# A gated SSM/MLP kernel: deeper buffer rings for the last stage, and a re-planned order of all engines

## The chip, the cores and the metric

The kernel runs on one core of a Trainium2 chip. The metric is the time of one execution in device microseconds (us), lower is better: the median of 8 runs. Beside it there is one execution that was profiled by the hardware; all durations below come from that one.

## What is computed

A token sequence of 2048 rows and 640 columns, `A_q`, goes through two branches that are mixed by a gate per row. Cut to what matters:

```python
g = sigmoid((A_q * gate_w).sum(-1))
# branch A: long convolution of kv with ssm_k, by FFT
k_shift = sum of 4 shifted copies of A_k, each times a column of A_shift_k
kv = k_shift * A_v
y  = irfft(rfft(kv padded) * rfft(ssm_k padded))[:2048] + kv * ssm_D
a  = A_q * y
# branch B: token-shift mixer, then an MLP
h  = gelu(layernorm(A_q) @ w1)
x1 = A_q + shifted(h) @ w2          # quarters of h shifted by +1, -1, +2, -2 rows
b  = x1 + gelu(layernorm(x1) @ w3) @ w4
out = g * a + (1 - g) * b
```

## The kernel before

The rows are held as 128 partitions times 16 slabs (slab `s` is a [128 x 640] tile). The FFT is written as matmuls with tables, in two steps with a trip through DRAM between them, because the second step needs the rows in another layout.

The work is cut into some 600 nodes with names. `ORDER` (line 85 of the file) is one long string that lists all of them, each with its engine and the number of the ring slot for each of its buffers: `y0/V/1/0` is node `y0` on VectorE with slot 1 of one ring and slot 0 of another. A ring is a small set of buffers; a node that takes a slot waits until the last user of that slot is done. The string was written by a planner that is not part of the kernel. The kernel just emits the nodes in this order, so that **each engine executes its own nodes in the order of the string**, one after the other, and a node that waits holds up everything behind it on its engine. P is TensorE, V is VectorE (DVE), A is ScalarE (ACT), G is GpSimd (POOL), S is SyncE (SP), which issues all DMAs.

The nodes that the text speaks of, with the lines of the profile:

- `st`, `rs`, `xn`, `xt` (L497 to L537): layer norm. `st` takes statistics (VectorE, or ScalarE L503), `rs` on POOL (L516 to L523) makes the factor, `xn` normalises (VectorE, L530), `xt` is a transposing DMA (L537).
- `W1`, `g1` (L574, L581), `mx` (L609 to L614, copies of a 32-partition part for the shifts), `W2`, `add` (L663, L670): the mixer. `W3`, `g2` (L749, L753), `W4`, `w4e` (L762, L768): the MLP in four chunks of 512 rows; `w4e` adds (1 - g) times the product into the slab `QX[:, s]`. `xo` scales `QX` by (1 - g) ahead of it (VectorE L682 or ScalarE L684).
- `h1`, `he`, `hw` and `x1`, `xe`, `xw`: the first step of the transform of `ssm_k` and of `kv` (L718, copies L320/L324, DMA to DRAM L727). `km`, `ka`, `kv` (L806, L811, L815, L818): the shifted products on VectorE that make `kv`; they read 1280 elements per partition from each of two SBUF operands.
- `m3i0` to `m3i5`, `m3b`, **`m3c`** (16 small POOL instructions, L432 to L448), **`m3d`** (VectorE, L452), `m3s` (ScalarE sine, L454), `m3n` (POOL, L456): a chain that computes the small table for the second step. `w4` (the load of W4, L733) and `tri` wait for `m3n`.
- `rh`, `rx` (DMA L862, back from DRAM), `h2`, `x2`, `pv` (TensorE L835), `h2e`, `x2e`, `ve` (copies out of PSUM), `sw` (DMA L878), `pq` (VectorE product L895), `vw` (DMA to DRAM L912): the second step, the product of the spectra and the inverse's first step, in four chunks of five.
- The **tail**: `rv` (L919) reads the inverse's input back from DRAM, eight DMAs of 640 KB; `rq` (L923) loads `A_q` again, eight of 320 KB; for each slab `iv` (TensorE, 4 matmuls, L931), `ye` (ScalarE, L941, PSUM to SBUF times g), `y` (VectorE, times q, L945), `ya` (VectorE, adds it into `QX`, L951) and `st` (DMA to the output, L953). `rv0` waits for all four `vw`.

In the tail `rv` has a ring of 4 slots, `rq` of 2, and the product buffer `GY` (written by `ye`) of 4. The last `W3`/`W4` nodes are put between the nodes of the trip to DRAM and of the tail, to fill TensorE.

Of the kernel before, what the change touches and what calls it, by code (L numbers as in the profile page):

```python
# [109 lines left out]
km0.1.1/V/0/0 km0.1.0/V/0/1 xo3/A ka0.1.1/V/0/0 m3i1/G mx2.3/G W2.6/P/6 ka0.1.0/V/1/0 add6/V/6 xt1.0.1/S/0/1 w3/S h1.8.0/P/0/2  # L110
he.8.0/A/0/2 kv2/V/0 W2.7/P/4 add7/V/4 m3c/G m3d/V m3s/A W2.9/P/2 add9/V/2 mx3.2/G xt1.0.2/S/0/0 W2.8/P/0 xt1.0.3/S/0/2
W3.0.7/P/6/0/0 g2.0.7/A/6/0 W3.0.8/P/7/0/1 g2.0.8/A/7/1 xo5/A add8/V/0 h1.15.0/P/4/0 W3.0.3/P/0/0/2 W3.0.4/P/1/0/0
W3.0.9/P/6/0/1 g2.0.4/A/1/0 he.15.0/A/4/0 W3.0.2/P/7/0/2 W3.0.5/P/1/0/0 g2.0.5/A/1/0 g2.0.9/A/6/1 st1.6/A mx3.3/G k1/S/1
# [874 lines left out]
```

## Time and profile before

| what | value |
|---|---|
| median of 8 runs (lowest, highest) | 232.05 us (229.82, 235.35) |
| the profiled execution's own time | 230.78 us |
| its span in the profile | 229.0 us |
| TensorE busy | 213.0 us, 93% of the span |
| VectorE, ScalarE, POOL busy | 189.3, 165.3, 60.8 us |
| granted TensorE clock | 0.99 of full speed |
| bytes moved by DMA | 65.9 MB, 288 GB/s on average |

The span runs from the first to the last instruction of the profile; the execution's own time has 1.8 us around it. The page divides the span into 40 slices with a digit for the busy share of each, follows the chain of work that ended last back from the end, and lists groups of equal instructions with the idle time before them and what ended it. A wait is named as "engine line waited for: total us, times, longest". The mean length of a matmul includes its way through the array; from one start to the next, 128x512 matmuls stand 0.216 us apart, and 128x320 ones 0.136 us.

### The profile page before, as it was taken

How to read it: one execution, taken by the hardware profiler on the slowest of the kernel's cores; microseconds unless marked ns; L12 is line 12 of the kernel's file. 1: busy time of each engine (PE TensorE's matmuls, PEld its weight loads, DVE VectorE, ACT ScalarE, POOL GpSimd, SP SyncE). 2: the span in 40 equal slices, each digit the busy share in tenths (PEclk: the TensorE clock that was granted, in tenths of full speed). 3: DMA queues.
4: the chain of work that ended last, by engine and by line, in shares of the span. 5: the costliest groups of instructions: out<-in, count | busy, mean ns of one | idle time of the engine just before them, and what ended most of it. 6: DMA issues, size and time to landing. Idle time of an engine off the chain costs nothing.

```text
span 229.0 us, 4443 instructions
## 1 busy us (share of the span) xinstructions
PE 213.0 (93%) x1626; PEld 124.7 (54%) x1641; DVE 189.3 (83%) x340; ACT 165.3 (72%) x252; POOL 60.8 (27%) x137
## 2 busy tenths in 40 slices
PE   6879999999899999999999999998999999999970
PEld 6747457565544567645566466432355554566740
DVE  8999989979999999999997668996658895066883
ACT  6899989899386653569987932998997884645630
POOL 2645765269997426500002210000000000000000
PEclk9999999999999999999999999999999999999997
DMA  7999979999996993999999999999999962799896
GB/s 210 371 391 297 331 165 254 196 260 320 261 402 195 374 295 79 241 243 230 301 304 382 315 284 326 332 239 387 302 350 309 376 234 100 216 406 356 270 372 235
DMA packets 53031, 65.90 MB, mean 288 GB/s; under 512 B 22545, under 2 KB 39698, under 8 KB 52625
## 3 DMA queue, kind: packets, MB, share of 16 engines
q1 hardware_dynamic: 53008, 65.61, 93.2%
q8 instruction: 13, 0.21, 0.4%
q14 instruction: 10, 0.07, 0.1%
HBM read 37.03 MB, written 18.35 MB: 242 GB/s over the span
## 4 chain that ended last, share of the span: by engine, by line
PE 54%; DVE 16%; DMA 12%; POOL 6%; issue 4%; SPq 3%; ACT 3%; DVEq 0%; POOLq 0%; ACTq 0%
PE PS L762 15%; PE PS L749 13%; PE PS L835 7%; PE PS L718 6%; PE PS L574 5%; PE PS L663 5%; DMA RG<-in_A_ssm_k_dram 5%; DMA CJ<-in_A_q_dram 4%; DVE RK L811 3%; DVE RK L815 3%; DMA RK<-GHD 3%; DVE QX L670 2%; DVE QX L768 2%; DVE RK L945 1%; POOL R L609 1%
## 5 line engine op out<-in xcount | busy, mean ns | idle before, releaser
L320 ACT CAST SX<-PS 128x640 bf16<-128x640 f32 (+1 forms) x62 | 46.5, 777 | 18.9 <-PE PS L835 10.9
L762 PE MATMUL PS<-W,RG 128*128 128x320 bf16 x384 | 56.2, 299 | 1.3 <-DVE QX L768 0.6
L749 PE MATMUL PS<-XNT,W 128*128 128x512 bf16 x229 | 54.9, 379 | 1.4 <-DVE KV L818 0.6
L762 PEld LDWEIGHTS <-RG 128*128 128x128 bf16 x384 | 36.6, 98 | 20.5 <-issue 6.9
L749 PEld LDWEIGHTS <-W 128*128 128x128 bf16 x240 | 22.6, 98 | 29.1 <-issue 5.5
L753 ACT ACTIVATE RG<-PS 128x512 bf16<-128x512 f32 x48 | 27.8, 606 | 8.7 <-PE PS L749 8.6
L768 DVE SCALAR_TENSOR_TENSOR QX<-PS,ZG,QX 128x320 bf16<-128x320 f32 x32 | 17.1, 544 | 13.7 <-PE PS L762 13.7
L895 DVE TENSOR_TENSOR SX<-SX,R 128x2048 bf16<-128x2048 bf16 x20 | 24.1, 1221 | 4.7 <-PE PS L835 1.9
L574 PE MATMUL PS<-XNT,R 128*128 128x512 bf16 x96 | 24.0, 379 | 1.3 <-DMA R<-in_B_w_dram 1.1
L718 PE MATMUL PS<-KV,F 128*128 128x320 bf16 x128 | 23.9, 299 | 0.1
L663 PE MATMUL PS<-R 128*128 128x320 bf16 x160 | 23.4, 299 | 0.0
L324 DVE CAST SX<-PS 128x640 bf16<-128x640 f32 (+1 forms) x22 | 19.9, 910 | 4.1 <-PE PS L718 2.4
L815 DVE TENSOR_TENSOR RK<-RK 128x1280 bf16<-128x1280 bf16 x24 | 20.6, 859 | 0.4
L941 ACT ACTIVATE RK<-PS,ZG 128x640 bf16<-128x640 f32 x16 | 11.8, 793 | 12.6 <-PE PS L931 7.4
L811 DVE TENSOR_TENSOR RK<-RK,CJ 128x1280 bf16<-128x1280 bf16 x24 | 20.1, 855 | 0.0
L663 PEld LDWEIGHTS <-R 128*128 128x128 bf16 x160 | 15.7, 98 | 6.4
L320 ACT CAST KV<-PS 128x1024 bf16<-128x1024 f32 x17 | 17.0, 1017 | 2.3 <-PE PS L835 2.2
L718 PEld LDWEIGHTS <-F 128*128 128x128 bf16 x128 | 12.2, 98 | 8.8
L574 PEld LDWEIGHTS <-R 128*128 128x128 bf16 x100 | 9.5, 98 | 10.3 <-DMA R<-in_B_w_dram 1.2
L530 DVE TENSOR_SCALAR XN<-QX,MV,RS 128x640 bf16<-128x640 bf16 x32 | 14.3, 463 | 0.4 <-POOL RS L523 0.4
L523 POOL TENSOR_TENSOR RS<-VE,NHALF 128x2 f32<-128x2 f32 x16 | 14.0, 875 | 1.3
L835 PEld LDWEIGHTS <-M 64*64 64x64 bf16 x320 | 7.5, 105 | 12.3 <-issue 7.0
(104 smaller groups left out, 286.0 us busy)
## 6 DMA issues: line engine op xcount, KB each, us to landing
GHD<-SX SPq DMA_DIRECT2D x8, 640.0 KB, 4.6
GXD<-SX SPq DMA_DIRECT2D x8, 640.0 KB, 4.5
RK<-GHD SPq DMA_DIRECT2D x4, 1280.0 KB, 8.5
RK<-GXD SPq DMA_DIRECT2D x4, 1280.0 KB, 6.3
R<-R SPq DMA_DIRECT2D x8, 640.0 KB, 6.3
VD<-KV SPq DMA_DIRECT2D x4, 1280.0 KB, 6.2
RK<-VD SPq DMA_DIRECT2D x8, 640.0 KB, 5.7
W<-in_B_w_dram SPq DMA_DIRECT2D x2, 1920.0 KB, 8.2
```

What stands on the lines that cost most here:

```text
L320: nc.scalar.copy(out=o, in_=i)
L574: nc.tensor.matmul(ps(pb), lhsT=lhsT, rhs=XNT[:, xb.idx, k, :], start=(k == 0), stop=(k == DT - 1))
L663: nc.tensor.matmul(ps(pb)[:, j, 0:DH], lhsT=gst_ap(k, s), rhs=W2[:, k, j * DH:(j + 1) * DH], start=(k == 0), stop=(k == DT - 1))
L718: nc.tensor.matmul(ps(pb)[:, j, 0:DH], lhsT=F1[:, s // 4, h, s % 4, :], rhs=src[:, s, ds], start=True, stop=not dterm)
L749: nc.tensor.matmul(ps(pb), lhsT=W3[:, k, f0 * P:(f0 + 1) * P], rhs=XNT[:, xb.idx, k, :], start=(k == 0), stop=(k == DT - 1))
L753: gns.append(pl.add("g2.%d.%d" % (c, f0), {A: act_p(512)}, lambda e, f0=f0, pb=pb, gb=gb: nc.scalar.activation(out=GTP[:, gb.idx, f0 % 4, ...
L762: nc.tensor.matmul(ps(pb)[:, 0:DH], lhsT=GTP[:, gbs[f // 4].idx, f % 4, i * P:(i + 1) * P], rhs=W4[:, f, j * DH:(j + 1) * DH], start=(f == ...
L768: nc.vector.scalar_tensor_tensor(out=x, in0=ps(pb)[:, 0:DH], scalar=OMG[:, s:s + 1], in1=x, op0=ALU.mult, op1=ALU.add)
L811: m = pl.add("km%d.%d.%d" % (c, u, j), {V: dve(2 * D, .52)}, lambda e, src=src, cj=cj, tb=tb: nc.vector.tensor_tensor(out=TMP[:, tb.idx].r ...
L815: prev = pl.add("ka%d.%d.%d" % (c, u, j), {V: dve(2 * D, .52)}, lambda e, tb=tb: nc.vector.tensor_tensor(out=acc, in0=acc, in1=TMP[:, tb.i ...
L835: nc.tensor.matmul(pt[64 * C:64 * C + 64, R, :], lhsT=M3[64 * R:64 * R + 64, m, :], rhs=rhs_fn(R, C), start=start, stop=stop)
L895: nc.vector.tensor_tensor(out=PQ[:, qb.idx], in0=XS[:, sb.idx].unsqueeze(1).to_broadcast([P, 2, 1024]), in1=HH[:, hhb.idx, u], op=ALU.mult)
```

## The change

Three rings of the tail get more slots, in memory that other tiles have left by then. `rv` goes from 4 to 7 (three in the space of the W3 weights), the product buffer `GY` from 4 to 8 (four in the space of the normalised, transposed inputs), and `rq` from 2 to 5 (three in the space of the transform table `F1`). A slot in borrowed space is free when its former readers are done: all `W3` matmuls, or all `x1` matmuls and the two `tri` transposes.

The planner was then run again, and **the whole string `ORDER` is another one**, from the first entry on. Every node is still there once. These change engine: one `cj` copy from ScalarE to POOL, `kz` and four of 16 `mx` copies from POOL to VectorE, four `xo` and one `te` from ScalarE to VectorE, and 43 of the copies out of PSUM one way or the other (`he`, `xe`, `ve`, `h2e`, `x2e`).

The diff; of the string only the lines that hold the places the text speaks of, first the old ones, then the new ones:

```diff
 ORDER = """
...
-he.8.0/A/0/2 kv2/V/0 W2.7/P/4 add7/V/4 m3c/G m3d/V m3s/A W2.9/P/2 add9/V/2 mx3.2/G xt1.0.2/S/0/0 W2.8/P/0 xt1.0.3/S/0/2
...
-x2e.1.0/A/0/0 pv.1.3/P/4/1/1 xt1.3.2/S/1/1 ve.1.3/A/4/1 xt1.3.1/S/1/2 xt1.3.0/S/1/0 W3.3.8/P/2/1/3 g2.3.8/A/2/3 rh2/S/1 rq1/S/1
...
-pq.3.2/V/2/0/0 W3.3.6/P/0/1/0 pv.3.0/P/6/1/1 pv.3.2/P/4/0/1 W3.3.0/P/1/1/1 ve.3.0/V/6/1 ve.3.2/A/4/1 vw3/S/1 W3.3.2/P/6/1/1
...
-rv0/S/0 iv0/P/4/0 iv1/P/6/0 ye0/A/4/0 y0/V/0/0 ya0/V/0 w4e10.1/V/2 ye1/A/6/1 y1/V/1/0 rv1/S/1 iv3/P/0/1 ye3/A/0/2 y3/V/2/1
...
-y6/V/1/1 ya7/V/3 W4.1.0/P/2/1/0/3 ya5/V/0 ya6/V/1 w4e1.0/V/2 iv8/P/4/0 iv9/P/6/0 W4.14.1/P/3/1/0/3 ye8/A/4/2 rv7/S/1 iv15/P/0/1
-ye15/A/0/3 iv14/P/4/1 ye14/A/4/0 W4.15.0/P/2/1/0/3 rv6/S/2 iv12/P/0/2 rq7/S/0 y15/V/3/0 rq4/S/1 rv5/S/3 st7/S st4/S y14/V/0/0
...
-st3/S st14/S w4e15.0/V/2 W4.15.1/P/4/1/0/3 w4e15.1/V/4 ya15/V/3 iv10/P/6/3 ye10/A/6/1 y10/V/1/0 ya10/V/1 st10/S iv11/P/0/3
-ye11/A/0/2 y11/V/2/0 ya11/V/2 st11/S st15/S W4.0.1/P/5/1/0/3 w4e0.1/V/5 st0/S y12/V/0/1 ya12/V/0 st12/S iv13/P/2/2 ye13/A/2/3
-y13/V/3/1 ya13/V/3 st13/S
...
+W1.2.4/P/0/0 st1.5/A W1.2.3/P/1/0 g1.2.3/A/1 h1.10.1/P/2/0 he.10.1/A/2/0 h1.10.0/P/4/0 he.10.0/A/4/0 g1.2.4/A/0 W1.2.0/P/7/0
...
+xt1.0.3/S/0/2 mx2.3/V gate0/V mx2.1/G W2.7/P/4 mx2.0/G km0.1.2/V/0/1 km0.1.1/V/0/0 ka0.1.2/V/1/0 ka0.1.1/V/0/0 m3c/G m3d/V
...
+g2.0.2/A/1/0 ka2.0.2/V/0/0 W3.0.10/P/0/0/2 W2.10/P/4 km2.0.1/V/0/1 add10/V/4 ka2.0.1/V/1/0 km2.0.0/V/0/0 ka2.0.0/V/0/0 kv8/V/0
+g2.0.10/A/0/2 W4.3.1/P/0/0/1/2 w4e3.1/V/0 W4.5.1/P/1/0/1/2 W4.5.0/P/2/0/1/2 W4.2.1/P/3/0/1/2 x1.2.0/P/6/0 W4.3.0/P/4/0/1/2
+xe.2.0/A/6/0 km2.1.3/V/0/0 w4e3.0/V/4 km2.1.2/V/0/1 st1.11/A W2.13/P/6 w4e5.1/V/1 w4e2.1/V/3 W4.4.0/P/0/0/1/2 w4e5.0/V/2
+W2.12/P/4 w4e4.0/V/0 add12/V/4 st1.10/A ka2.1.2/V/1/0 km2.1.1/V/0/0 W4.2.0/P/0/0/1/2 st1.12/A W3.1.10/P/1/1/3 w4e2.0/V/0
...
+g2.3.10/A/2/3 W3.3.8/P/3/1/3 x2.1.1/P/0/0/2 x2e.1.1/A/0/2 g2.3.8/A/3/3 rq1/S/1 rh2/S/1 x2.1.4/P/4/0/0 x2e.1.4/V/4/0 rq2/S/2
...
+g2.3.6/A/4/0 W3.3.3/P/2/1/1 g2.3.3/A/2/1 rq3/S/3 vw2/S/0 W3.3.1/P/3/1/1 g2.3.1/A/3/1 W4.0.0/P/2/1/0/3 w4e0.0/V/2
+W4.14.0/P/3/1/0/3 w4e14.0/V/3 w4e10.1/V/1 vw3/S/1 w4e13.1/V/0 W4.1.1/P/2/1/0/3 w4e1.1/V/2 rq7/S/4 rv0/S/0 iv1/P/6/0 ye1/A/6/0
+iv0/P/4/0 ye0/A/4/1 y0/V/1/0 y1/V/0/0 rv1/S/1 ya0/V/1 ya1/V/0 iv3/P/0/1 ye3/A/0/2 iv2/P/2/1 ye2/A/2/3 y3/V/2/1 W4.1.0/P/4/1/0/3
+y2/V/3/1 ya2/V/3 w4e1.0/V/4 rv3/S/2 iv7/P/6/2 ye7/A/6/4 y7/V/4/3 iv6/P/0/2 ye6/A/0/5 y6/V/5/3 ya3/V/2 rv2/S/3 iv5/P/2/3
+ye5/A/2/6 ya6/V/5 iv4/P/6/3 y5/V/6/2 ye4/A/6/7 y4/V/7/2 ya4/V/7 rv4/S/4 W4.15.0/P/0/1/0/3 w4e15.0/V/0 iv9/P/4/4 ye9/A/4/1
+rv7/S/5 ya5/V/6 rq4/S/0 y9/V/1/0 ya7/V/4 iv8/P/2/4 ye8/A/2/0 y8/V/0/0 ya9/V/1 ya8/V/0 rv5/S/6 rv6/S/0 rq5/S/1 rq6/S/3
+iv14/P/6/5 ye14/A/6/3 y14/V/3/4 ya14/V/3 W4.14.1/P/0/1/0/3 w4e14.1/V/0 iv15/P/4/5 ye15/A/4/2 iv11/P/2/6 y15/V/2/4 ya15/V/2
+ye11/A/2/5 y11/V/5/1 ya11/V/5 st5/S st7/S st1/S st6/S st4/S st14/S st3/S iv10/P/6/6 iv12/P/4/0 iv13/P/0/0 ye12/A/4/7 y12/V/7/3
+ya12/V/7 st2/S st9/S st11/S st8/S st12/S ye10/A/6/6 y10/V/6/1 ya10/V/6 st10/S W4.15.1/P/2/1/0/3 w4e15.1/V/2 st15/S ye13/A/0/4
+y13/V/4/3 ya13/V/4 st13/S W4.0.1/P/3/1/0/3 w4e0.1/V/3 st0/S
...
-    VX = RK[:, 0:10240].rearrange("p (b h t d) -> p b h t d", b=4, h=2, t=2)
-    GY = RK[:, 10240:12800].rearrange("p (b d) -> p b d", b=4)
-    QR = CJ.rearrange("p (b t) d -> p b t d", b=2)
+    VX4 = RK[:, 0:10240].rearrange("p (b h t d) -> p b h t d", b=4, h=2, t=2)
+    VX3 = W34[:, 0:7680].rearrange("p (b h t d) -> p b h t d", b=3, h=2, t=2)
+    GY4 = RK[:, 10240:12800].rearrange("p (b d) -> p b d", b=4)
+    GY8 = XNT.rearrange("p b k t -> p (b k t)").rearrange("p (b d) -> p b d", b=8)
+
+    def vx(b):
+        return VX4[:, b.idx] if b.idx < 4 else VX3[:, b.idx - 4]
+
+    def gy(b):
+        return GY4[:, b.idx] if b.idx < 4 else GY8[:, b.idx - 4]
+    CJQ = CJ.rearrange("p (b t) d -> p b t d", b=2)
+    F1Q = F1.rearrange("p g h t d -> p (g h t d)")[:, 0:3840].rearrange("p (b t d) -> p b t d", t=2, d=D)
+
+    def qr(b):
+        return CJQ[:, b.idx] if b.idx < 2 else F1Q[:, b.idx - 2]
...
-    r_vx = Ring("vx", 4)
-    r_gy = Ring("gy", 4)
-    r_qr = Ring("qr", 2)
+    r_vx = Ring("vx", 7)
+    r_gy = Ring("gy", 8)
+    r_qr = Ring("qr", 5)
...
-        ldhx = pl.dma("rh%d" % cc, lambda e, hx=hx, rd=rd: rd(GHD, e, hx), 8 * P * D * 2, hwr + ldxs[:max(0, cc - 1)], [hx], ndesc=1024)
+        ldhx = pl.dma("rh%d" % cc, lambda e, hx=hx, rd=rd: rd(GHD, e, hx), 8 * P * D * 2, hwr + ldxs[:max(0, cc - 1)], [hx], iss=800.0, ndesc=1024)
...
-        ldx = pl.dma("rx%d" % cc, lambda e, xb=xb, rd=rd: rd(GXD, e, xb), 8 * P * D * 2, xwr, [xb], ndesc=1024)
+        ldx = pl.dma("rx%d" % cc, lambda e, xb=xb, rd=rd: rd(GXD, e, xb), 8 * P * D * 2, xwr, [xb], iss=800.0, ndesc=1024)
...
-        xb = Buf(r_vx, x2pe)
+        xb = Buf(r_vx, x2pe + w3pe)
-            out=VX[:, xb.idx], in_=VD.rearrange("h p t d -> p h t d")[:, :, 2 * c:2 * c + 2, :]), 2 * 2 * P * D * 2, vwr, [xb],
+            out=vx(xb), in_=VD.rearrange("h p t d -> p h t d")[:, :, 2 * c:2 * c + 2, :]), 2 * 2 * P * D * 2, vwr, [xb],
-        qb = Buf(r_qr, kall)
-        lq = pl.dma("rq%d" % c, lambda e, qb=qb, c=c: nc.sync.dma_start(out=QR[:, qb.idx], in_=q3[:, 2 * c:2 * c + 2, :]),
+        qb = Buf(r_qr, kall + xpe + i1n)
+        lq = pl.dma("rq%d" % c, lambda e, qb=qb, c=c: nc.sync.dma_start(out=qr(qb), in_=q3[:, 2 * c:2 * c + 2, :]),
-            pb, yb = Buf(r_ps, (), 2), Buf(r_gy, kall)
+            pb, yb = Buf(r_ps, (), 2), Buf(r_gy, kall + w3pe)
-                        nc.tensor.matmul(ps(pb)[:, j, 0:DH], lhsT=I1[:, s // 4, h, s % 4, :], rhs=VX[:, xb.idx, h, s % 2, j * DH:(j + 1) * DH],
+                        nc.tensor.matmul(ps(pb)[:, j, 0:DH], lhsT=I1[:, s // 4, h, s % 4, :], rhs=vx(xb)[:, h, s % 2, j * DH:(j + 1) * DH],
-                nc.vector.scalar_tensor_tensor(out=GY[:, yb.idx].rearrange("p (j d) -> p j d", j=2), in0=ps(pb)[:, :, 0:DH],
+                nc.vector.scalar_tensor_tensor(out=gy(yb).rearrange("p (j d) -> p j d", j=2), in0=ps(pb)[:, :, 0:DH],
-                                               in1=QR[:, qb.idx, s % 2, :].rearrange("p (j d) -> p j d", j=2),
+                                               in1=qr(qb)[:, s % 2, :].rearrange("p (j d) -> p j d", j=2),
-                nc.scalar.activation(out=GY[:, yb.idx].rearrange("p (j d) -> p j d", j=2), in_=ps(pb)[:, :, 0:DH], func=ACT.Copy,
+                nc.scalar.activation(out=gy(yb).rearrange("p (j d) -> p j d", j=2), in_=ps(pb)[:, :, 0:DH], func=ACT.Copy,
-                nc.vector.tensor_tensor(out=GY[:, yb.idx], in0=GY[:, yb.idx], in1=QR[:, qb.idx, s % 2, :], op=ALU.mult)
+                nc.vector.tensor_tensor(out=gy(yb), in0=gy(yb), in1=qr(qb)[:, s % 2, :], op=ALU.mult)
-                out=QX[:, s, :], in0=QX[:, s, :], in1=GY[:, yb.idx], op=ALU.add), [y, xo[s]], [yb])
+                out=QX[:, s, :], in0=QX[:, s, :], in1=gy(yb), op=ALU.add), [y, xo[s]], [yb])

```

The `iss=800.0` that two DMA nodes get is a number for the planner; it changes nothing in what the kernel emits.

## The prediction

> **What bounds the kernel now.** I read the page first (shares), then the busy time in stretches, then the chain that ended last, then the timelines of VectorE and POOL where the chain turns.
>
> ```profile
> span 229.0 us, 4443 instructions
> ...
> PE 213.0 (93%) x1626; PEld 124.7 (54%) x1641; DVE 189.3 (83%) x340; ACT 165.3 (72%) x252; POOL 60.8 (27%) x137
> ```
>
> TensorE is the bound nearly everywhere: the starts of its instructions give some 207 us of pure work (48 W3 groups at 1.08, 32 W4 at 1.63, 20 W1 at 1.08, 16 W2 at 1.36, and so on), so no order can go much below 215. Next the stretches (columns: PE, PE loads, DVE, ACT, POOL busy; clock; DMA share; GB/s):
>
> ```profile
> 62.00:95.00 33.00, 31.35 (x190) 18.77 (x193) 32.28 (x53) 19.09 (x38) 20.86 (x35) 1.00 0.85 273
> 95.00:126.00 31.00, 30.79 (x183) 18.02 (x185) 28.81 (x48) 25.03 (x45) 2.11 (x7) 1.00 1.04 287
> ...
> 190.00:202.00 12.00, 11.85 (x75) 6.13 (x76) 1.85 (x3) 5.56 (x9) 0.00 (x0) 1.00 0.61 206
> 202.00:226.00 24.00, 19.25 (x138) 12.98 (x136) 18.74 (x42) 11.84 (x16) 0.00 (x0) 1.00 0.96 345
> ```
>
> From 62 to 95 VectorE is full (32.28 of 33) and TensorE loses 1.65; from 95 to 126 TensorE has no gap worth naming, so whatever lateness it has at 97 it keeps. In the tail (202 to 226) no engine is full. What sets the pace there is in the chain (start, length, what):
>
> ```profile
> 211.31 3.84 DMA CJ<-in_A_q_dram
> 215.24 0.91 DVE RK L945 x2
> 216.16 4.93 DMA CJ<-in_A_q_dram
> 221.19 0.50 DVE RK L945
> ```
>
> Two loads of q (`rq`) cost 8.8 us of the chain: with two slots, a load starts only when the products with the slab pair before are done, and takes its 4 to 5 us to land.
>
> **The tail, step by step.** The new `rq` order loads q0, q1, q2, q3, q7 ahead of `rv0`; only q4, q5, q6 follow, each long before its product. So that wait goes. What is late next? Times as if all before the tail were unchanged:
> - `rv0` lands at 201.53 (issued 197.29). After the last `pv` TensorE has, before, 7 W3 and 2 W4 groups (7 x 1.08 + 2 x 1.63 = 10.8, 190.99 to 201.9); the new order has a third W4 (`W4.1.1`), so `iv1` starts at 203.6, 1.6 after its data.
> - `iv1` 0.54, `ye1` and `ye0` 0.79 each: `y0` starts at 205.85. Then VectorE has 16 `y`, 16 `ya` and 5 `w4e`, 37 instructions. A single one is recorded at 0.49, but 20 of them in the stretch 210 to 220 take 8.61, 0.43 each. At 0.445 the 37 take 16.5: end at 222.3. In the profile the last `ya` ends at 225.45. Gain **3.1**.
> - TensorE from 203.6: 16 x 0.54 + 5 x 1.63 = 16.8, end 220.4, plus a `w4e` 221.0: covered by VectorE. ScalarE: 16 x 0.79 from 204.2, covered.
> - SP issues the 16 stores behind `rq6`, at 0.41 each; the first is ready at about 214, so they keep up. From the last `ya` to the end of the span 3.55 us pass before, and I keep them.
> - DMA: 8 `rv` (5.24 MB), 3 `rq` (0.98) and the stores (2.62), 8.84 MB in all. Row first: `rv0` and `rv1` land 1.72 apart and later ones 1.63, some 397 GB/s; from 199.9 the stream ends at 222.2, hidden by VectorE. The Trainium skill (SBUF — State Buffer, "Summary: rules for kernel authors") says to reckon transfers between HBM and SBUF at about 358 GB/s. By that the stream ends at 224.6 against a last landing that I expect at 225.0: the cover is nearly gone. This trace moved 402 GB/s in its best slice, so I take the row.
> Bounds: 4.4 gained if VectorE is never the bound (221.0), 1.0 if every second product waits for its copy.
>
> **The rest of the string.** It is new from the first entry, and what the tail gains can be lost ahead of it. I went by landmarks: sum the recorded lengths of all that stands ahead of an instruction on its engine in each order (a moved instruction at the mean of its kind), and ask when the old order had that much work done. Most agree: `kv14` has 120.4 us ahead (before 121.2), starting at 114.0 (114.8); `h2`, `x2`, `pv` stand within 1 us on TensorE; switches between its 64x64 and 128x128 work are 44 in both. The loads that TensorE waits for in the first 20 us are issued in the same order. Those parts I cost at 0 (0.5 either way). Not equal are four places.
>
> 1. *VectorE waits for POOL at `m3d`.* POOL's timeline (start, length, what):
>
> ```profile
> 57.35 0.66 POOL L437 TENSOR_SCALAR W<-W 128x1 f32<-128x1 f32 x1
> ...
> 62.76 0.35 POOL L447 CAST W<-W 128x192 int32<-128x192 f32 x1
> ```
>
> and VectorE's timeline, in brackets its idle time and what ended it:
>
> ```profile
> 63.14 0.26 DVE L452 TENSOR_SCALAR W<-W 128x192 int32<-128x192 int32 x1 [0.38 <-POOL W L447]
> ```
>
> `m3c` runs on POOL from 54.88 and its cast ends at 63.11, 8.2 us; `m3d` comes right then (0.38 wait). In the new order `m3d` has 60.4 of work ahead instead of 66.0: its turn is at 57.4. POOL is earlier too. `st1.5` on ScalarE moves up some 3 us, so `rs1.4` starts near 46.5 (before 49.06), takes 3.0 (the two such runs took 2.3 and 3.6), then `mx2.1` and `mx2.0` at 0.65: `m3c` starts at 50.8 and its cast ends at 59.0. Wait 1.6, **+1.2** net. Behind `m3d` stand `km0.1.0`, `add6` and all later `w4e`; `m3s`, `gate1` and the `g2` copies wait on ScalarE.
> The lock rule speaks against me. A one-column POOL instruction takes 0.66 here; the two-column L516 takes 0.22 to 0.31 while VectorE is on other work. The skill (SBUF — State Buffer, "Who interferes with whom") says that a VectorE instruction with two SBUF inputs and a POOL instruction that reads SBUF exclude each other for a whole instruction. From 50.8 on VectorE would have only such products, 0.82 each; half of one plus 0.25 for each of 15 instructions is 9.9, so the wait is 2.9 net instead of 1.2. I take the row, since its stretch was full of the same products. Bounds: -0.4 (no wait) and +5.3 (POOL reaches `m3c` at 54.88 as before).
>
> 2. *A PSUM slot.* `W4.3.1`, `W4.4.0`, `W4.2.0`, `W3.1.8` all use slot 0, each behind the `w4e` of the one before. `w4e4.0` has 97.9 of VectorE work ahead, so it ends at 93.5; `W4.2.0` has 83.6 of TensorE work ahead, so it could start at 92.5. At `W3.1.8` the lateness is 93.5 + 1.63 + 1.08 + 0.54 = 96.8 against 96.0, **+0.8** (0 to 2). Item 1 adds to this one to one, as VectorE has no idle time to absorb it.
>
> 3. *Fewer POOL copies.* Between 63.7 and 68.7 POOL made five `mx` copies, up to 1.10 each where 0.61 is usual, and `ka1.0.2` on VectorE took 1.65 instead of 0.83. Three remain there: **-0.6** (-1 to 0).
>
> 4. *SP's queue.* `rq2` now goes ahead of `vw0` and `rh3`. From 151.8 to 168.9 5.57 MB landed without a pause, 327 GB/s; 0.33 MB more is 1.0 later. `rh3` had 0.5 to spare (landed 164.8, used 165.35): **+0.5** (0 to 1.2). `rh2`, for which TensorE waited 1.0, has `rq1` ahead of it now but one transpose less: 0 (-1 to +0.9). `rq3` ahead of `vw2` and `rq7` ahead of `rv0` find the queue slack (share 0.61): 0, up to 0.9 without that slack.
>
> Sum: -3.1 + 1.2 + 0.8 - 0.6 + 0.5 = **-1.2**, span 227.8. The profiled execution took 230.78 (span 229.0), the median is 232.05, 3.05 above the span; I keep that distance: 230.8.
>
> **The rivals.**
> - *The middle costs nothing* (POOL reaches `m3c` two microseconds earlier, slot 0 is free in time). For it: POOL idles 4.95 before 47.57, so it can be earlier; and the 0.5 that TensorE waited for the W4 load goes, as `m3n` comes earlier. Then 229.0 - 3.1 - 0.5 = 225.4, median 228.4. Against it: ScalarE is 90% busy up to 60.
> - *Slower: VectorE stands at `m3d`.* If POOL comes to `m3c` no earlier than before, VectorE loses 5.3: -3.1 + 5.3 + 0.8 - 0.6 + 0.5 = +2.9, median 235.0. It outweighs the tail from a net wait of 2.4, and by over 1% from 4.7. For it: `rs1.4`, `mx2.1` ahead of `m3c` hang on ScalarE's last statistics and on `g1.2.4`, whose work ahead is greater than before (40.2 against 39.1). Against it: three small POOL nodes have left its way.
> - *The change does little in the tail*: products wait for copies or DMA instead of q, gain 1.0, and the middle costs its 1.9: +0.9, median 233.0. For it: DMA was at 0.96 already.
>
> **How the numbers follow.** Likeliest, 0.36: 230.8, own range 229.6 to 232.4. Middle free 0.24, slower at `m3d` 0.30, little tail 0.10. About 1% (2.3 us) is what a measurement of this kernel can tell from none. Faster by over 1% (under 229.7): 0.2 of the first, 0.9 of the second, 0.29. Slower by over 1% (above 234.4): 0.7 of the third and a little of the others, 0.25. Between: 0.46. Range 228.0 to 235.6: the middle case's better half and the slow one's worse half stay out, under 0.2.
>
> **What would show it.** No wait of L957 (`y`) for q; `y0` some 2 us after the first `iv`, VectorE dense for 16.5 us from there. A wait of `m3d` for POOL of about 1.6 near 58. TensorE waiting for `w4e` between 87 and 94. I am wrong if `m3d` does not wait or waits 5, or if the tail from the first `iv` to the end is not about 22 us.

## The result, and the profile after

The changed kernel takes 229.60 us (median of 18 runs, 228.99 to 232.03). Beside it the kernel before took 232.62 (53 runs). The ratio is **0.9914** (95% interval 0.989 to 0.9938), 2.0 us less: inside the 1% that the prediction set as the bound. The two medians lie 3.0 us apart, because that of the kernel before holds slower executions as well (the highest took 280.96), and the ratio is taken without them. The profiled execution took 230.24 us with a span of 228.4; the median span of all its runs is 227.8.

All lines of the code after the string are 12 higher than before (`y` is L957, `ya` L963, `m3d` L464). The page:

```profile
span 228.4 us, 4433 instructions
...
PE 213.6 (94%) x1625; PEld 125.0 (55%) x1641; DVE 189.5 (83%) x347; ACT 162.4 (71%) x250; POOL 62.1 (27%) x133
```

The busy times in stretches (columns: PE, PE loads, DVE, ACT, POOL; clock; DMA share; GB/s), the tail from 205 on:

```profile
62.00:95.00 33.00, 31.45 (x183) 18.61 (x186) 32.10 (x58) 16.25 (x33) 14.06 (x23) 0.95 0.95 295
95.00:126.00 31.00, 30.64 (x183) 18.06 (x186) 27.50 (x45) 25.97 (x48) 5.38 (x10) 1.00 0.84 241
...
190.00:205.00 15.00, 14.34 (x92) 7.42 (x91) 4.02 (x6) 6.69 (x10) 0.00 (x0) 1.00 0.66 219
205.00:228.00 23.00, 17.59 (x128) 12.24 (x126) 17.14 (x39) 11.49 (x16) 0.00 (x0) 0.93 0.85 316
```

From 62 to 95 VectorE is as full as before and TensorE stands idle for 1.55 us. One number is another: the clock, 0.95 instead of 1.00. A narrow window shows where it is lost:

```profile
64.00:68.00 4.00, 4.00 (x12) 1.47 (x11) 3.93 (x13) 3.49 (x6) 1.79 (x4) 0.57 0.99 402
```

For 3.41 us from 64.45 on, the profile gives TensorE half its clock: eight 128x512 matmuls there start 0.427 us apart instead of 0.216, which is 1.7 us more. Just ahead TensorE had stood idle for 2.09 us. More on this at the end. (The 0.93 in the last row is of no account: TensorE's last matmul starts at 222.29, and the clock falls at 224.88.)

The tail is VectorE's now: 16.55 us of work in one piece, as its timeline says (start, length, what; in brackets the idle time ahead):

```profile
207.59 0.89 DVE L957 TENSOR_TENSOR RK<-RK,CJ 128x640 bf16<-128x640 bf16 x2 [1.50 <-ACT RK L953]
...
223.59 0.55 DVE L780 SCALAR_TENSOR_TENSOR QX<-PS,ZG,QX 128x320 bf16<-128x320 f32 x1
```

From 207.59 to 224.14 there are 37 instructions and 16.55 us; no bracket names q. SP's timeline shows what came behind:

```profile
215.01 10.61 SPq L965 DMA_DIRECT2D out_dram<-QX  x16
```

The last of the 16 stores went out at 225.21, 1.1 us after VectorE was done, and the span ended 3.2 us after that. One of the stores held SP up; the summary of their line gives the shortest, the median and the longest issue in ns:

```profile
L965 SPq DMA_DIRECT2D out_dram<-QX x16: 332/405/2217, 215.0 to 225.2; - x16
```

The 2217 ns are `st2`'s, from 219.45; the eight stores behind it came late.

To compare tails I take one point that all kernels share, 0.2 us ahead of the last `pv`. Behind that `pv` TensorE has the same work in every order: 7 `W3`, 8 `W4` and 16 `iv`, some 29.3 us. From the point to the end of the span it is 38.75 us before (190.25 to 229.0) and 36.96 after (191.44 to 228.4).

And the place in the middle, on POOL, VectorE and ScalarE in turn:

```profile
45.14 4.11 POOL L531 TENSOR_SCALAR MV<-ST 128x2 f32<-128x2 f32 x1
...
53.29 0.31 POOL L444 CAST W<-W 128x5 f32<-128x5 int32 x1
...
59.91 0.34 POOL L459 CAST W<-W 128x192 int32<-128x192 f32 x1
```

```profile
60.29 0.26 DVE L464 TENSOR_SCALAR W<-W 128x192 int32<-128x192 int32 x1 [2.19 <-POOL W L459]
```

```profile
60.59 0.46 ACT L466 ACTIVATE W<-W,BPI 128x192 f32<-128x192 int32 x1 [2.08 <-DVE W L464]
61.06 1.28 ACT L648 ACT_TABLE_LOAD   x1
62.35 0.21 ACT L648 ACTIVATE ZG<-ZH 128x16 f32<-128x16 bf16 x1
```

`rs1.4`'s first instruction took 4.11 us where 0.24 is usual, `m3c` began at 53.29, and VectorE stood 2.19 us at `m3d`. ScalarE stood behind it, and then paid a table load that the kernel before does not have here, because `gate1` (a tanh) now comes behind the sine of `m3s`.

### The profile page after: what moved, and what is told of

Read it like the earlier page. It is cut to its first block, busy times and chain, and to the rows that moved or that the text cites. A ratio compares the mean times of both kernels' runs of the same rounds, so it can differ in the third digit from the quotient of the medians.

```text
span 228.4 us, 4433 instructions
## 1 busy us (share of the span) xinstructions
PE 213.6 (94%) x1625; PEld 125.0 (55%) x1641; DVE 189.5 (83%) x347; ACT 162.4 (71%) x250; POOL 62.1 (27%) x133
## 4 chain that ended last, share of the span: by engine, by line
PE 67%; DMA 9%; DVE 8%; POOL 7%; issue 3%; SPq 2%; ACT 1%; ACTq 0%; DVEq 0%; POOLq 0%
PE PS L774 21%; PE PS L761 18%; PE PS L847 8%; PE PS L675 7%; DMA RG<-in_A_ssm_k_dram 5%; PE PS L730 5%; DMA RK<-GHD 4%; PE PS L586 4%; PE PS L943 4%; POOL MV L531 2%; DVE RK L827 2%; DVE RK L823 2%; DVE QX L682 1%; POOL RS L535 1%; POOL W L457 1%
## 5 line engine op out<-in xcount | busy, mean ns | idle before, releaser
L332 ACT CAST SX<-PS 128x640 bf16<-128x640 f32 (+1 forms) x65 | 47.7, 765 | 25.4 <-PE PS L730 13.3
L761 PE MATMUL PS<-XNT,W 128*128 128x512 bf16 x228 | 57.4, 388 | 2.7 <-DVE QX L682 2.1
L774 PEld LDWEIGHTS <-RG 128*128 128x128 bf16 x384 | 36.5, 98 | 19.6 <-issue 4.7
L730 PE MATMUL PS<-KV,F 128*128 128x320 bf16 x128 | 24.9, 299 | 0.1
L336 DVE CAST SX<-PS 128x640 bf16<-128x640 f32 (+1 forms) x19 | 18.1, 966 | 3.5 <-PE PS L730 1.9
L827 DVE TENSOR_TENSOR RK<-RK 128x1280 bf16<-128x1280 bf16 x24 | 19.8, 826 | 0.4
L332 ACT CAST KV<-PS 128x1024 bf16<-128x1024 f32 x18 | 18.0, 1029 | 2.1 <-PE PS L847 2.0
L823 DVE TENSOR_TENSOR RK<-RK,CJ 128x1280 bf16<-128x1280 bf16 x24 | 19.4, 817 | 0.0
L531 POOL TENSOR_SCALAR MV<-ST 128x2 f32<-128x2 f32 x8 | 7.2, 902 | 39.5 <-DVE QX L682 39.2
L515 ACT ACTIVATE RG<-QX 128x640 bf16<-128x640 bf16 x16 | 11.8, 737 | 4.7 <-issue 4.6
L682 DVE SCALAR_TENSOR_TENSOR QX<-PS,QX 128x640 bf16<-128x640 f32 x16 | 13.0, 819 | 2.4 <-PE PS L675 2.3
```

Source lines behind the costliest of these rows:

```text
L332: nc.scalar.copy(out=o, in_=i)
L336: nc.vector.tensor_copy(out=o, in_=i)
L730: nc.tensor.matmul(ps(pb)[:, j, 0:DH], lhsT=F1[:, s // 4, h, s % 4, :], rhs=src[:, s, ds], start=True, stop=not dterm)
L761: nc.tensor.matmul(ps(pb), lhsT=W3[:, k, f0 * P:(f0 + 1) * P], rhs=XNT[:, xb.idx, k, :], start=(k == 0), stop=(k == DT - 1))
L774: nc.tensor.matmul(ps(pb)[:, 0:DH], lhsT=GTP[:, gbs[f // 4].idx, f % 4, i * P:(i + 1) * P], rhs=W4[:, f, j * DH:(j + 1) * DH], start=(f == ...
L823: m = pl.add("km%d.%d.%d" % (c, u, j), {V: dve(2 * D, .52)}, lambda e, src=src, cj=cj, tb=tb: nc.vector.tensor_tensor(out=TMP[:, tb.idx].r ...
```

## Experiments

The question had two halves. What is the new tail worth, and which part of it: q's early loads and slots, the two other rings, or the new order? And what does the new order ahead of it cost, and is it the wait at `m3d`? My theory was the prediction's: the tail gains 3, by q; the middle gives 1.9 back, most of it at `m3d`. The rivals: the other rings carry the gain; or the middle costs nothing; or ScalarE, with its new table load, is what TensorE waits for.

Each ratio below is to the kernel before on the same chip; the kernels were not all measured on one chip, so the ratios are to be compared, not the medians. In kernels whose string is one line shorter every later line number is one lower.

| kernel | median us | ratio (95%) | from the point at the last `pv` to the end, us |
|---|---|---|---|
| before | 232.62 | 1 | 38.75 |
| changed | 229.60 | 0.9914 (0.989 to 0.9938) | 36.96 |
| e1_old_tail | 235.31 | 1.0156 (1.010 to 1.0211) | 42.3 |
| e2_new_tail | 229.95 | 0.9927 (0.9897 to 0.9958) | 38.0 |
| e3_q_only | 235.46 | 1.0135 (1.0077 to 1.0193) | |
| e4_m3d_later | 228.16 | 0.9863 (0.9815 to 0.9911) | 36.5 |
| e5_new_tail2 | 227.97 | 0.9834 (0.9794 to 0.9874) | 35.9 |
| e6_q_ring2 | 230.86 | 0.9952 (0.9915 to 0.9989) | 37.7 |
| e7_q_ring_new_order | 229.96 | 0.9922 (0.9888 to 0.9955) | 37.2 |
| e10_gate1 | 229.95 | 0.9908 (0.9872 to 0.9943) | 35.8 |
| e9_w3_early | 229.55 | 0.9919 (0.988 to 0.9958) | 36.3 |
| e12_w3_stores | 229.13 | 0.9872 (0.9835 to 0.9909) | 35.4 |
| e13_new_tail2_stores | 228.51 | 0.9836 (0.9801 to 0.9871) | 36.0 |
| e8_m3d_later_stores | 228.39 | 0.9867 (0.9807 to 0.9928) | 35.5 |

### The tail taken back: e1_old_tail

```diff
-rq3/S/3 ... rq7/S/4 rv0/S/0 iv1/P/6/0 ye1/A/6/0 iv0/P/4/0 ... st0/S
+rv0/S/0 iv0/P/4/0 iv1/P/6/0 ye0/A/4/0 ... rv4/S/0 rq2/S/0 ... st13/S
```

> The new order up to the first read back (rv0), then the old tail: old node order and slots, rings of 4, 4 and 2, q2, q3, q7 loaded in the tail again. Theory (the tail's rings gain about 3 us, the new middle gives part of it back): this loses the gain and keeps the cost, so about 3 us above the new kernel, 1.003 to 1.006 times the old one. Rival (the 0.86% come from the re-planned rest, the rings bring nothing): 0.991 as the new kernel.

Against the changed kernel it loses 2.4%, 5.6 us, about twice what my theory said, and the rival said a gain. VectorE's timeline still has the wait for q, and TensorE's one for a read-back that had to wait for its slot:

```profile
219.37 0.49 DVE L957 TENSOR_TENSOR RK<-RK,CJ 128x640 bf16<-128x640 bf16 x1 [3.92 <-DMA CJ<-in_A_q_dram]
```

```profile
216.94 2.32 PE L943 MATMUL PS<-RK,I 128*128 128x320 bf16 x8 [2.67 <-DMA RK<-VD]
```

(In this group TensorE also ran at half its clock, which lasted 3.41 us from 216.48 on: the eight matmuls took 2.32 us instead of 1.25.) The new head hands over with one W4 group more already done (`W4.1.1`, 1.63 us) and is later itself, so the first `iv` comes at 204.9 instead of 202.1. An old tail, paced by loads that start only when a product frees a slot, does not shorten for having less TensorE work: it starts 2.8 later and its last `ya` ends 3.7 later. What the tail is worth depends on what stands ahead of it, so e1 does not give its price by itself. The next runs do that from the old head.

### The tail alone: e2_new_tail, then e5_new_tail2

```diff
-W4.0.0 w4e13.1 W4.14.0 w4e14.0 w4e0.0 rv0/S/0 iv0 iv1 ye0 y0 ya0 w4e10.1 ...
+W4.0.0 w4e13.1 W4.14.0 w4e14.0 w4e0.0 xo15 w4e10.1 W4.1.1/P/2 w4e1.1 rv0/S/0 iv1 ye1 iv0 ...
```

> The old order up to rv0, with q2, q3, q7 loaded just behind the DMAs vw2 and vw3, then the new tail with its rings of 7, 8 and 5. Theory: the tail's gain of about 3 us without the middle's cost of about 1 us: 0.984 to 0.988 times the old kernel, better than the new one. Rival (the rings bring nothing): 0.998 to 1.002.

A gain, but less than expected, and TensorE's timeline told that I had built a wait of my own:

```profile
203.97 1.79 PE L773 MATMUL PS<-W,RG 128*128 128x320 bf16 x12 [1.92 <-DVE QX L779]
```

`W4.1.1` took the PSUM slot of `W4.10.1`, whose `w4e` stood behind that of `W4.14.0`. The second try moves `w4e10.1` forward:

```diff
-W4.0.0 w4e13.1 W4.14.0 w4e14.0 w4e0.0 xo15 w4e10.1 W4.1.1/P/2 w4e1.1 rv0/S/0
+W4.0.0 w4e10.1 w4e13.1 W4.14.0 w4e14.0 w4e0.0 xo15 W4.1.1/P/2 w4e1.1 rv0/S/0
```

> Once more the old order up to the first read-back and the new tail, as in e2_new_tail, but with W4.1.1 in a PSUM slot that is free: in e2 it took the slot of W4.10.1, whose w4e stood behind that of W4.14.0, and TensorE waited 1.9 us for it just ahead of the first inverse product. Here w4e10.1 and w4e13.1 come first. Theory (the tail gains by its rings and its order, the stores give back 0.75): the first inverse product moves from 205.5 to about 203.7, span 226.0 to 227.0, ratio to the kernel before 0.983 to 0.989. Rival (the old head cannot feed the new tail any faster, the wait only changes its name): span 227.7 to 228.5, ratio 0.991 to 0.995.

As the theory had it: 0.9834, 3.9 us less than the kernel before (2.9 to 4.8), and 0.8% less than the changed kernel. The new tail on the old head is worth more than the whole change.

### Which part of the tail: e3_q_only, e6_q_ring2, e7_q_ring_new_order

```diff
-vw2/S/0 ... vw3/S/1 ... rv4/S/0 rq2/S/0 ... rq3/S/1 ... rv6/S/2 rq7/S/0 rq4/S/1 rv5/S/3 ... rq5/S/0 ... rq6/S/1
+vw2/S/0 rq2/S/2 rq3/S/3 ... vw3/S/1 rq7/S/4 ... rv6/S/2 rq4/S/0 rq5/S/1 rv5/S/3 rq6/S/2
```

> The old order throughout, with one part of the change alone: the q ring has 5 slots and its eight loads are placed early (q2, q3 behind vw2, q7 behind vw3, q4 and q5 behind the last but one read back, q6 behind the last). The other rings stay at 4. Theory: the two waits for q of the old chain (8.8 us of it) go, but the products then wait for the 4 product buffers and the reads back for their 4 slots, so only a part of 3 us is gained: 0.990 to 0.996. Rival (q alone is the whole gain of the tail): 0.984 to 0.988. Rival (nothing): 1.0.

This kernel is not what was meant. The `y` nodes name the slot of q too, and theirs were the old ones, so the buffer had two slots after all: by the string, loads 2, 3 and 7 go into pairs that have not been used yet, so that some products would take another q. Its time says only what hurried loads into two slots cost: `rq4` stood in SP's queue until 215.22, `rv5` behind it. With the slots of the `y` nodes set as well:

```diff
-y5/V/0/0 y4/V/2/0 y7/V/3/1 y6/V/1/1 y15/V/3/0 y14/V/0/0 y8/V/2/1 y9/V/1/1
+y5/V/0/2 y4/V/2/2 y7/V/3/3 y6/V/1/3 y15/V/3/4 y14/V/0/4 y8/V/2/0 y9/V/1/0
```

> The old order with the ring of q alone at five slots: loads 2 and 3 behind vw2, 7 behind vw3, 4 and 5 behind the seventh read-back, 6 behind the last; the y nodes name the new slots. (In e3_q_only they still named the old ones, so that run had two slots and hurried loads.) Rings of the inverse inputs and of the products stay at four. Theory A (the waits for q were the tail's loss, as the chain says): no wait of L957 for q, last ya at 222.5 to 224.3 instead of 225.5, ratio 0.987 to 0.995. Theory B (the other two rings or the new order of VectorE carry the gain; without them the waits change their name to ScalarE's copy and to the read-backs): ratio 0.997 to 1.003.

Theory A in the time, but only just (0.9952, 1.1 us, interval 0.3 to 2.0), and B in the mechanism: q is waited for no more, and VectorE waits for ScalarE's copy in the same place. In the kernel before, VectorE's timeline has two waits for q, 2.79 us in all:

```profile
210.24 1.03 DVE L945 TENSOR_TENSOR RK<-RK,CJ 128x640 bf16<-128x640 bf16 x2 [1.83 <-DMA CJ<-in_A_q_dram]
215.24 0.89 DVE L945 TENSOR_TENSOR RK<-RK,CJ 128x640 bf16<-128x640 bf16 x2 [0.96 <-DMA CJ<-in_A_q_dram]
```

In place of the first, here:

```profile
211.22 0.49 DVE L957 TENSOR_TENSOR RK<-RK,F 128x640 bf16<-128x640 bf16 x1 [2.52 <-ACT RK L953]
```

The copy was late because the read-backs came next: `iv5` waited for `rv2` (landed 206.52), `iv6` for `rv3` (208.17), and the copy stood behind theirs. So q's waits in the old order were 1.1 us of real loss, not the 8.8 that its loads fill in the chain, nor the 2.8 that VectorE stood for them. The other way round, the new order with only q's ring deeper:

```diff
-rv4/S/4 rv7/S/5 rv5/S/6 rv6/S/0 ye7/A/6/4 ye6/A/0/5 ye5/A/2/6 ye4/A/6/7 ye9/A/4/1 ...
+rv4/S/0 rv7/S/1 rv5/S/2 rv6/S/3 ye7/A/6/1 ye6/A/0/0 ye5/A/2/3 ye4/A/6/2 ye9/A/4/0 ...
```

> The changed kernel with the rings of the inverse inputs and of the products put back to four slots and only q's at five; the order of all engines stays the new one. By the times of the changed kernel a slot is free 0.5 us or more before its next copy in 11 of 12 cases, and a read-back that is issued 5 us later still finds the transfers of those before it under way. Theory A (q's ring and the order carry the gain): within 0.3% of the changed kernel, ratio to before 0.989 to 0.995, VectorE still dense for about 16.5 us. Theory B (the two other rings carry it): ratio 0.998 or more, VectorE waits for ScalarE's copies, or TensorE for read-backs.

0.9922 against 0.9914: the same. VectorE's timeline has the same solid block, now with slots used again at once:

```profile
206.77 0.89 DVE L956 TENSOR_TENSOR RK<-RK,CJ 128x640 bf16<-128x640 bf16 x2 [1.50 <-ACT RK L952]
...
223.02 0.55 DVE L779 SCALAR_TENSOR_TENSOR QX<-PS,ZG,QX 128x320 bf16<-128x320 f32 x1
```

From 206.77 to 223.57, 16.8 us. **In this order, two of the three rings that the change makes deeper do nothing that the time shows.** Five slots for q, and an order in which q, copies and products come when they are needed, are the gain: 1.1 us the slots alone in the old order, another 2.7 (e5 against e6) the new order of the tail. e5 has the two other rings as well; that they do nothing there is taken over from e7. The new order of the tail with two slots for q was not run. It loads q2, q3 and q7 before the first product, which two slots do not allow as it stands, but another order might have done with fewer than five.

### The middle: e4_m3d_later and e10_gate1

```diff
-m3c/G m3d/V m3s/A m3n/G k1/S/1 mx2.2/G mx3.1/V km0.1.0 mx3.0/G ka0.1.0 W2.6 add6 add7 W2.8 add8 gate1/A gate2
+m3c/G gate1/A k1/S/1 mx3.1/V km0.1.0 ka0.1.0 W2.6 add6 m3d/V m3s/A m3n/G mx2.2/G mx3.0/G add7 W2.8 add8 gate2
```

> The new kernel with one place mended: m3d on VectorE five nodes later (behind add6), and the gate's tanh on ScalarE ahead of the sine m3s and not behind it, which also saves one table load of 1.28 us there. Theory (VectorE's wait of 2.2 us for POOL and the table load are what the new middle costs): TensorE's wait before W3.0.1 and W3.0.11 shrinks by 1.5 to 2.5 us and the time by 1 to 2 us: 0.983 to 0.987 times the old kernel. Rival (later pins of TensorE on w4e near 94 hide it): 0.990 to 0.992 as the new kernel.

0.9863: 1.2 us less than the changed kernel by the ratios, though their intervals just meet. VectorE waits 0.67 at `m3d` instead of 2.19:

```profile
62.11 0.26 DVE L463 TENSOR_SCALAR W<-W 128x192 int32<-128x192 int32 x1 [0.67 <-POOL W L458]
```

The traces bear it out. From `W2.9` to `W3.1.8` TensorE loses 3.7 to 4.0 us beyond its own work in the four kernels with the long wait (changed, e1, e7, e10), and 2.5 to 2.9 in the four in which `m3d` comes later (e4, e8, e9, e12). But two things were moved, `m3d` and `gate1`, and the table load went too. So `gate1` alone:

```diff
-m3c/G m3d/V m3s/A m3n/G ... W2.8 add8 gate1/A gate2
+m3c/G gate1/A m3d/V m3s/A m3n/G ... W2.8 add8 gate2
```

> The changed kernel with one node moved: gate1 (a tanh on ScalarE) ahead of m3s (the sine) instead of behind it. m3d keeps its place and its wait of 2.2 us for POOL. Theory A (in the first 10 us after the mixer ScalarE is what TensorE waits for, and the table load of 1.28 us that the tanh needs behind the sine is most of it): no table load at the tanh, the losses of TensorE at W3.0.4, W3.0.11 and h1.15.1 (2.1 us together) shrink to under 0.8, ratio to before 0.984 to 0.988, as e4_m3d_later. Theory B (the wait of m3d is what counts, since add6 stands behind it on VectorE): the loss between W2.9 and W3.0.1 stays at 1.8, ratio 0.989 to 0.993.

Theory B: 0.9908, the time of the changed kernel. ScalarE's timeline shows why:

```profile
57.72 0.28 ACT L647 ACTIVATE ZG<-ZH 128x16 f32<-128x16 bf16 x1
58.02 1.28 ACT L465 ACT_TABLE_LOAD   x1
...
64.17 1.28 ACT L764 ACT_TABLE_LOAD   x1 [2.43 <-DVE QX L681]
66.23 0.60 ACT L764 ACTIVATE RG<-PS 128x512 bf16<-128x512 f32 x1 [0.77 <-PE PS L760]
```

The tanh has no load of its own now, but ScalarE stands idle for 2.43 us instead, for VectorE's `add6`. VectorE's wait at `m3d` is 2.20 as before, and `add6` hangs on it. The losses of TensorE behind `W3.0.1`, which theory A laid to ScalarE (in the changed kernel's trace), were its clock in the main: here too it was at half for 3.41 us, from 64.44 on.

### Is it VectorE or TensorE there: e9_w3_early

In e4 TensorE stood 1.18 us ahead of W3, for transposes that came behind the W3 load in the DMA queue.

```diff
-xt0.3.0/S/1/1 ... v1/S ... hw6/S/1 ... xt1.0.0/S/0/2 ... w3/S ... xt1.0.1/S/0/0
+xt0.3.0/S/1/1 w3/S ... hw6/S/1 ... xt1.0.0/S/0/2 v1/S ... xt1.0.1/S/0/0
```

> e4_m3d_later with one DMA moved: the load of W3 (1.97 MB) goes ahead of hw6 and xt1.0.0, and v1 goes behind xt1.0.0. In e4 TensorE lost 1.45 us ahead of W3.0.1, waiting for the transposes of the second layer norm, whose data came behind that load in the queue (issued 50.4 to 56.6, landed 60.2 to 61.5). Theory A (what TensorE loses is lost): that wait goes, time 1.2 us below e4, ratio to before 0.978 to 0.983. Theory B (from 62 to 97 VectorE is the bound, 34.5 of 35 us busy; TensorE only comes earlier to the next PSUM slot): the wait goes, the loss at W4.2.0 and W3.1.10 grows by about as much, W3.1.8 stays at 96 and the ratio at 0.984 to 0.989.

No better than the changed kernel, 0.9919, and 1.3 us above e4 by the ratios (the intervals overlap); of use for that. TensorE's wait for transposes went, and VectorE got one, as the load of W3 now held up the transpose `xt1.0.0` (landed at 56.60 instead of 52.87), whose source buffer `xn1.5` needs:

```profile
56.62 0.45 DVE L541 TENSOR_SCALAR XN<-QX,MV,RS 128x640 bf16<-128x640 bf16 x1 [1.43 <-DMA XNT<-XN]
```

TensorE now waits for VectorE's adds there (0.73 and 0.32 us, behind L681) instead of for DMA: in this stretch VectorE is the bound. At `W3.1.8` TensorE was 4.27 us later than at `h1.0.0`, beyond its own work, against 3.20 in e4. Of this difference of 1.1 us some 0.7 have another cause: `hw6` stood behind the moved load too (landed at 55.91 instead of 52.18), a copy of ScalarE waited 1.31 us for it, and `W1.3.2` for the copy. So the run shows that an earlier W3 does not help, but not what a wait of VectorE costs.

### The stores: e12_w3_stores, e13_new_tail2_stores, e8_m3d_later_stores

```diff
-st5 st7 st1 st6 st4 st14 st3 ... st2 st9 st11 st8 st12 ... st10 ... st15 ... st13 ... st0
+st2 st1 st3 st6 st4 st5 st7 st9 st8 ... st14 ... st11 ... st12 ... st10 ... st15 ... st13 ... st0
```

> e9_w3_early with the 16 stores in the order in which their slabs become ready (2, 1, 3, 6, 4, 5, 7, 9, 8, 14, 11, 12, 10, 15, 13, 0). In the changed kernel the first store in the queue was one of a slab that was ready at 215.0 while four others had been ready since 210.6 to 213.2; SP then issued one each 0.45 to 0.5 us and put out the last store 1.1 us after VectorE's last instruction. Theory: the last store goes out 0.2 us after VectorE's end, end of the span 3.3 to 3.5 us after it instead of 4.3, 0.7 to 1.0 us below e9. Rival (the queue takes a store only when the DMA eight before it has landed, and the read-backs land as before): gain under 0.3.

> e5_new_tail2 (old order up to the first read-back, new tail) with the stores in the order of readiness, as in e12. Theory: 0.7 to 1.0 us below e5, ratio to before 0.979 to 0.982, and the end of the span 3.3 to 3.5 us after VectorE's last instruction. Rival: gain under 0.3, ratio 0.983 to 0.986. It also says which head is the better one once both have the same tail: by the times so far the old head with the new tail and e4 are within 0.2 us.

> e4_m3d_later (the changed kernel with m3d and m3s behind add6, and gate1 ahead of m3s) with the stores in the order of readiness, as in e12; the load of W3 stays where the changed kernel has it. If the two gains add, 0.9 below e4: ratio to before 0.979 to 0.984, span 225.6 to 226.2. If the stores give nothing here, as in e13: ratio 0.984 to 0.988.

Against e9, e12 is lower by 0.47%, 1.1 us, in line with its theory (the intervals overlap). But e13 is level with e5 and e8 with e4. In the traces the end of the span lies 3.2 and 3.4 us behind the start of VectorE's last instruction in e12 and e8, and 4.2 and 4.3 in e9 and e4; in e13 it is 4.2 again.

What differs is less the order than one slow store. In e13 the issue of `st8` took 1.85 us (from 220.38), in e9 and e4 that of `st2` 2.03 and 1.77, in e12 that of `st11` 1.34. In e8 none is long:

```profile
L964 SPq DMA_DIRECT2D out_dram<-QX x16: 332/344/592, 212.4 to 224.1; - x16
```

Nor in e10, which has the old order of stores: there the distance is 3.7. So of the 1 us some 0.3 may be the order, and the rest is whether one issue takes 1.3 to 2.4 us instead of 0.4, as in ten of the 14 traces. What makes it long stays open, and with two of three pairs level in time, so does the gain by the stores. What else held SP in e8 is in its waits (engine, line, for what: us, times, longest):

```profile
SPq L964 <- DMA RK<-VD: 1.2, 1, 1.2
SPq L964 <- DMA W<-VD: 1.1, 1, 1.1
```

Stores that wait for read-backs which they do not use: `st5` went out at 217.03, 0.06 after `rv6` had landed, `st7` 0.06 after `rq5`, `st9` 0.06 after `rq6`. Each is the DMA eight places ahead in the queue. In these programs being ready is not enough for a store: the DMA eight places ahead must have landed.

No combination beats e5_new_tail2 (0.9834): the string of the kernel before up to the first read-back, and the tail of the changed kernel. It and e13 are faster than both kernels, clear of the intervals. e4, e8 and e12 lie within e5's interval, so which of these is the best is not told.

## Why the prediction was right

Its likeliest case (230.8, within 1% of before) came: 229.6, 0.5% under it. The number alone does not tell it from the first rival, "the middle costs nothing" (228.4): 229.6 lies 1.2 us from both, at the lower edge of the case's own range (229.6 to 232.4), and the ratio of 0.9914 only just keeps it inside the 1%. It is the wait at `m3d`, 2.19 us where that rival had none, that decides. Step by step:

**The tail.** The working was right nearly to the digit where it used rows of VectorE: from `y0` 37 instructions at 0.445, 16.5 us, measured 16.55. `y0` came 2.25 us after the first `iv`, as predicted. The DMA stream was hidden, as the row said: `rv0`, issued at 199.12, landed 4.2 later; the loads were all in by 218.4 and the stores behind them by 227.1. The 397 GB/s of the row held (`rv0` and `rv1` 1.65 apart, 655 KB), against the 358 of the Trainium skill (SBUF — State Buffer, "Summary: rules for kernel authors"). Failed: "so they keep up", of SP and the stores. `st2`'s issue took 2.22 us instead of 0.41, and the distance from VectorE's last work to the end is 4.2 us, not 3.55. From the first `iv` to the end it is 23.0 us, predicted about 22. Gain of the tail: predicted 3.1, measured 3.9 (2.9 to 4.8) with the old head; last `pv` to end 2.8 less in e5's trace, 1.8 in the changed kernel's.

What the prediction did not have is why the tail before was slow. It took the two loads of q in the chain (8.8 us) as what goes. e6 shows that without them the read-backs and the copies wait nearly as long; e7 that the copies' ring was deep enough once the order was another. The sum was still right, because it did not subtract the waits but asked what would be the bound next and counted its instructions.

**Item 1, `m3d`.** Predicted net +1.2, a wait of 1.6; measured wait 2.19, and +1.2 by e4's ratio against the changed kernel's (the intervals overlap; in the traces e4 and e8 gather 1.1 us less lateness between `h1.0.0` and the last `pv` than the four runs with the wait). That the sum came out is in part luck. Its terms were wrong and made up for each other in part: `rs1.4` began at 45.1 instead of 46.5 and took 6.3 us instead of 3.0, and `m3c` took 7.0 instead of 8.2. The long `rs1.4` is the lock that the prediction weighed and set aside. From 44.71 to 49.17 VectorE's instructions stand without a gap, most of them products of two SBUF operands, and POOL's L531 ended at 49.25, with the first pause:

```profile
48.36 0.81 DVE L823 TENSOR_TENSOR RK<-RK,CJ 128x1280 bf16<-128x1280 bf16 x1
49.97 0.16 DVE L609 COPY ZG<-PS 128x4 f32<-128x4 f32 x1 [0.80 <-PE PS L600]
```

The prediction read the rule of the Trainium skill (SBUF — State Buffer, "Who interferes with whom") as half a VectorE instruction of waiting for each POOL instruction. Here the wait was as long as the whole run. All kernels with this head show it at the same place, but they have the same instructions there, so that is one case and no proof of a rule. And it is not always so: from 54.95 to 58.10 VectorE made four such products without a gap, and POOL's `m3c` got on between them, slowly:

```profile
55.86 1.56 POOL L457 TENSOR_SCALAR W<-W 128x64 f32<-128x64 f32 x1
```

What lets POOL in at one place and not at the other stays open. For `m3c` the rule so read gave 9.9 and the row 8.2; it took 7.0, since its first half fell beside small instructions of VectorE, and its end beside a VectorE that waited.

**Unforeseen:** the table load at `gate1`. e10 shows that it cost nothing that can be seen, since ScalarE waited for VectorE there anyway. And the clock: the prediction put it at nothing, and in the profiled execution the half clock cost TensorE 1.7 us right behind the wait. By the mean clock of each execution this is common: of 18 executions of the changed kernel five have 0.997 or more and take 229.2 us on average, eleven have 0.988 or less and take 230.0. Where the clock was lost in those that were not profiled is not on record.

**Item 2, the PSUM slot,** +0.8: TensorE did not wait there in the changed kernel. It had lost its time earlier (2.09 idle ahead of W3, and 1.7 by the half clock in the next 5 us), so the slot was free when it came. In e4, without that loss, 0.77 us of wait stand at `W4.2.0`. The prediction added the two; by these traces they are one delay, paid at one place or the other. Between `W2.9` and `W3.1.8` TensorE became 3.93 us later than its work, before 2.75: +1.2 for items 1 to 3, predicted +1.4. But this agreement may be chance: e5, e6 and e13, which have the old head, lose 3.6 to 4.0 us in the same stretch.

**Item 4, SP's queue,** +0.5: between `h2.1.1` and the last `pv` 3.2 us were lost, before 3.4. No cost can be seen; six traces of the one old head differ by 2.2 us there.

**The head as a whole:** predicted +1.9. By the ratios 0.8%, 1.9 us (changed kernel and e7 against e5 and e13, which have the same tail). The traces say less, 0.3: lateness gathered between `h1.0.0` and the last `pv` is 7.1, 6.8, 8.2, 8.1, 7.0 and 8.4 in the six kernels with the old head (before, e2, e3, e5, e6, e13), and 8.4, 7.3, 7.6 and 8.4 in the four with the new one (changed, e1, e7, e10). Single traces differ by more than what is looked for, so how much of the 1.9 lies outside `m3d` stays open.

**The distance to the median.** The sum gave a span of 227.8, and the median span of the changed kernel's runs is 227.8. The prediction then added the 3.05 us between the profiled span of before and its median. Of these 1.8 lie around any span; the other 1.27 were there only because the profiled execution of before was one of the faster ones. That term alone makes the 1.2 us by which the prediction is too high. The sum met the median span in part by luck, for it started from that fast execution: against the kernel before at its usual pace the change gave 2.0 us (0.9914), where the sum has 1.2.

## What to carry to other kernels

A chain of waits names what ended each wait last, not what would be saved: before costing a wait as gain, ask what is ready when at the same place; here 8.8 us of q in the chain were 1.1 in the time. A wait of the engine that bounds the kernel can cost more than its length, as its clock may fall with it. Deeper rings are worth nothing where the old slot is free in time, which the due times of the trace tell beforehand (e7); the order that a ring allows can be worth more than the ring. And when a planner writes the whole order anew for a local change, put the old order back around the change and time that: here it had the lowest ratio of all.

## What the hardware showed that I had not expected

- TensorE's granted clock fell to half for 3.41 us in eight of the 14 traces, each time within 1.1 us of the end of a wait of TensorE of 1.76 to 2.67 us. Four other waits of 1.89 to 2.12 us (two in e1, one each in e2 and e7) did not bring it, and no shorter wait did. In five traces (e3, e8, e9, e12, e13) it fell at the second transpose, which waits for the first loads (0.42 to 2.59 us in the 14 traces, with the same loads in the same places): the wait and the clock together make over 2 us between two executions, so a single trace can't tell a change of 1 us in the span.
- A POOL instruction on 128 x 2 elements took 4.11 us (in e4 4.12, in e9 4.11) under an unbroken run of VectorE instructions, two of them with a single tensor as operand; it ended with the run. Under another such run, 10 us later, POOL was let in.
- A table load can stand on either side of a wait: in e10 the sine's came at 58.02, ahead of 1.99 us of waiting, and the next one's 1.28 us at 64.17 only after 2.43 us of idle ScalarE.
- SP held a ready store back until the DMA eight places ahead had landed, and sent it 0.06 us later (`st5`, `st7`, `st9`, `st8` in e8).
- The issue of one store took 1.3 to 2.2 us in nine traces and 2.4 in e7; in the other four (e3, e6, e8, e10) none took 0.9.
